# A fused attention and two-MLP kernel: the fill's first eviction, first k load and warm-up matmuls rearranged

## The chip, the cores and the metric

The kernel runs on one core of a Trainium2 chip. The metric is the device time of one execution in microseconds (us); lower is better. A core has engines that work side by side, each through its own queue in order: TensorE (PE in the rows; PEld is its loading of weights), VectorE (DVE), ScalarE (ACT), GpSimd (POOL) and SyncE (SP), which here only issues DMAs.

## The reference, cut to what matters

```python
def _attn_ref(q, k, v):                       # (2, 12, 448, 64) each
    scores = scale * np.matmul(q, k.transpose(0, 1, 3, 2))
    scores = np.where(mask, -1000000000.0, scores)      # causal
    scores = scores - np.max(scores, axis=-1, keepdims=True)
    attn = np.exp(scores)
    attn = attn / (np.sum(attn, axis=-1, keepdims=True) + 1e-09)
    return np.matmul(attn, v).astype(np.float32)
...
def reference(**kwargs):
    ...
    attn_out = _attn_ref(**attn_kwargs)
    x = np.ascontiguousarray(attn_out.transpose(0, 2, 1, 3)).reshape(B * S, H * D)
    x = _moe_ref(x=x, **moe_kwargs)           # silu(x @ w_in) @ w_out, 768 -> 2048 -> 768
    return _moe2_ref(x=x, **moe2_kwargs)      # softmax-linear unit, layer norm, 768 -> 1024 -> 768
```

Attention over 24 heads comes first, then two feed-forward layers over its 896 rows.

## The kernel before

Attention works on 12 pairs of heads, one pair to an iteration `i` of the loop at L342; the loop is software-pipelined. In iteration `i` the scores of pair `i` are computed (`scores`, TensorE, L117 and L109), their row maxima taken (`maxes`, VectorE, L128), and their exponentials with row sums (`exps`, ScalarE, L134). A pair has seven such units, in the order of `UNITS`. One iteration later the pair is normalised (`recip` and `norm`, VectorE and GpSimd, L138 to L146). Two iterations later (`TL = 2`, the pair is called `r`) it is transposed block by block on TensorE into PSUM (`transp`, L157, five groups `g` of up to four blocks) and evicted to SBUF (`evict`: groups 0, 1 and 4 by ScalarE, L175; groups 2 and 3 by VectorE, L173). Three iterations later the product with v follows (`pv`, L186), and one later the result is split into a high and a low part. The schedule is manual: every engine executes in the order in which the code issues.

PSUM holds the transposed groups in a ring of four buffers, tag "x" of the pool `psx`. The warm-up's tile `wp` and the product's tile use the same ring, so group 4 can be transposed only when group 0 has been evicted.

After the loop come four large matrix products on TensorE, with operands split into float32r high and low parts (three matmuls for one product); their weights are streamed in, unpacked and split by the other engines while TensorE works.

The fill is the stretch from the start until the loop runs full. It opens with two memsets on VectorE (L310 clears 448 columns of `xl`, L311 a query tile), `WARM` = 7 matmuls on the cleared columns whose result is not used (L314; 128 weight columns and 448 moving columns, float32r), and `load_pair(0)`, in which SP issues q (L86), k (L87) and two small query tails (L89). The first scores stand behind the warm-up in TensorE's order.

Of the kernel before, what the change touches and what calls it, by code (L numbers as in the profile page):

```python
# [8 lines left out]
F32 = mybir.dt.float32  # L9
# [6 lines left out]
B, H, S, D = 2, 12, 448, 64  # L16
# [12 lines left out]
RAWS = 4  # L29
LAG = 6  # L30
TL = 2
WARM = 7
FEEDS = (8, 10, 11, 12, 12)
GD = (0, 1, 1, 3)
XS = 3
# [7 lines left out]
def fused(ctx, tc, qT, kT, vv, vt, w1, w2, w3, w4, gl, out):  # L43
    nc = tc.nc
    PS = bass.MemoryType.PSUM

    def pool(name, bufs=1, **kw):
        return tc.alloc_tile_pool(name=name, bufs=bufs, **kw)
# [9 lines left out]
    xl = act.tile([128, KD, T], F32R, name="xl", tag="al")  # L58
    g_h, g_l = [None, None], [None, None]

    with tc.manual_schedule():
# [19 lines left out]
        def load_pair(p):  # L81
            b, hp = divmod(p, NP)
            k = att.tile([128, S], F32, name="k32", tag="k32", bufs=QB)
            q = att.tile([128, QC * 128], F32, name="q32", tag="q32", bufs=QB)
            v = att.tile([128, 2, NKB, D], F32, name="v32", tag="v32", bufs=8)
            nc.sync.dma_start(q, qT[b, hp, :, :QC * 128])  # L86
            nc.sync.dma_start(k, kT[b, hp])  # L87
            for j in range(2):
                nc.sync.dma_start(q3s[p % QB][64 * j:64 * j + 64, j], qT[b, hp, 64 * j:64 * j + 64, QC * 128:])  # L89
            raws[p] = (k, q, v)  # L90
# [28 lines left out]
        def ep(p, u):  # L119
            return es[p % EB][:, AT[u]:AT[u] + 4].rearrange("q b k -> q (b k)")[:, :wide(u[1])]  # L120

        def maxes(p, u):
            if p not in st:
                st[p] = att.tile([128, 4, 7], F32, name="st", tag="st", bufs=4)
            o, m = ep(p, u), (mask3 if u[1] == 3 else mask)[:, S - wide(u[1]):]
            if u[1] == 3:
                o, m = (a.rearrange("q (z k) -> q z k", z=2) for a in (o, m))
            nc.vector.tensor_tensor_reduce(  # L128
                o, scs[p, u[0], u[1]], m, -SCALE, 3.0e38,
                ALU.add, ALU.min, st[p][:, 0, COL[u]:COL[u] + 1])  # L130

        def exps(p, u):
            n = COL[u]
            nc.scalar.activation(ep(p, u), ep(p, u), AF.Exp, bias=st[p][:, 0, n:n + 1], scale=-1.0,  # L134
                                 accum_out=st[p][:, 1, n:n + 1])

        def recip(p):
            nc.vector.tensor_scalar(st[p][:, 2], st[p][:, 1], 1e-9, None, ALU.add)  # L138
            nc.vector.reciprocal(st[p][:, 3], st[p][:, 2])

        def norm(p, u, eng):
            r = st[p][:, 3, COL[u]:COL[u] + 1]
            if eng is nc.gpsimd:
                eng.tensor_tensor(ep(p, u), ep(p, u), r.to_broadcast([128, wide(u[1])]), ALU.mult)  # L144
            else:
                eng.tensor_scalar(ep(p, u), ep(p, u), r, None, ALU.mult)  # L146
# [7 lines left out]
        def transp(p, g):  # L154
            t = psx.tile([128, 4, 128], F32, name="tr", tag="x")
            for n, (j, c, kb) in enumerate(GROUPS[g]):
                nc.tensor.transpose(t[:, n], es[p % EB][:, AT[j, c] + kb], ident)  # L157
            trs[p, g] = t

        def evict(p, g):  # L160
            if g == 0:
                aT[p] = att.tile([128, NKB, 2, S], F32, name="aT", tag="aT")
            t, a = trs.pop((p, g)), aT[p]
            if g < 2:
                src, dst = t[:, :QC].rearrange("k c q -> k (c q)"), a[:, 0, g, :QC * 128]
            elif g < 4:
                w = 128 * (4 - g)
                src = t.rearrange("k c q -> k (c q)")[:, :2 * w].rearrange("k (j q) -> k j q", j=2)
                dst = a[:, g - 1, :, QC * 128 - w:QC * 128]
            else:  # L170
                src, dst = t.rearrange("k b (j q) -> k b j q", j=2), a[:, :, :, QC * 128:]
            if g in (2, 3):
                nc.vector.tensor_copy(dst, src)  # L173
            else:
                nc.scalar.activation(dst, src, AF.Copy)  # L175
# [14 lines left out]
        def pv_hi(p):  # L190
            b, hp = divmod(p, NP)
            nc.scalar.activation(xh[:, hp, b * S:b * S + S], pvs[p][:, :S], AF.Copy)

        def pv_lo(p):
            b, hp = divmod(p, NP)
            sl = slice(b * S, b * S + S)
            nc.vector.tensor_tensor(xl[:, hp, sl], pvs[p][:, :S], xh[:, hp, sl].bitcast(F32), ALU.subtract)
# [69 lines left out]
        def feed():  # L267
            m = fed[0]
            fed[0] += 1
            at = lambda a: order[a] if a < len(order) else None  # L270
            if m + 1 < len(order):
                conv_a(*order[m + 1])
            for _ in range(2):
                if len(pend) >= lag[0]:
                    finish(pend.pop(0))
            if m < len(order):
                n, c = order[m]
                conv_b(n, c, x3 if n == 3 else xs, at(m + 1))
                pend.append(m)
            if m + RAWS < len(order):  # L280
                load_w(*order[m + RAWS])
# [25 lines left out]
            nc.vector.tensor_copy(g_h[b][:, f], sg)  # L307
            nc.gpsimd.tensor_tensor(g_l[b][:, f], sg, g_h[b][:, f].bitcast(F32), ALU.subtract)  # L308

        nc.vector.memset(xl[:, 0, :S].bitcast(F32), 0.0)  # L310
        nc.vector.memset(q3s[0], 0.0)  # L311
        wp = psx.tile([128, 512], F32, name="pv", tag="x")
        for _ in range(WARM):
            nc.tensor.matmul(wp[:, :S], xl[:, 0, :128], xl[:, 0, :S], start=True, stop=True)  # L314
        load_pair(0)
        nc.gpsimd.memset(mask, 0.0)
        blk = mask[:, S - 128:]
# [24 lines left out]
        for i in range(NP2 + TL + 2):  # L342
            live = i < NP2
            n, r, p, x = i - 1, i - TL, i - TL - 1, i - TL - 2
            doN, doT, doP, doX = (0 <= a < NP2 for a in (n, r, p, x))
            if doX:
                pv_hi(x)
            if doN:
                exps(n, UNITS[6])
            if live:  # L350
                for _ in range(FEEDS.count(i)):
                    feed()
                for c in (2, 0, 1, 3):
                    scores(i, c)
                for u in UNITS[:2]:
                    maxes(i, u)
                for u in UNITS[:2]:
                    exps(i, u)
            if i == 1:
                for u in UNITS[2:4]:  # L360
                    maxes(i, u)
            late = ()
            if doN:
                recip(n)
                dve = [u for u in KEYS if u[1] < 2] if n == 0 else KEYS if n == NP2 - 1 else KEYS[-1:]
                for u in KEYS:
                    if u not in dve:
                        norm(n, u, nc.gpsimd)
                if n == NP2 - 1:
                    for u in dve:  # L370
                        norm(n, u, nc.vector)
                else:
                    late = dve
            if doX:
                pv_lo(x)
            if live and i != 1:
                for u in UNITS[2:4]:
                    maxes(i, u)
            if doT:
                for g in range(4):  # L380
                    transp(r, g)
                evict(r, 0)
                transp(r, 4)
                evict(r, 1)
            if live:
                for u in UNITS[2:4]:
                    exps(i, u)
                for u in UNITS[4:6]:
                    maxes(i, u)
            if doT:  # L390
                evict(r, 4)
            if doP:
                for z in range(NKB):
                    pv(p, z)
            if live:
                for u in UNITS[4:6]:
                    exps(i, u)
                maxes(i, UNITS[6])
            if doT:
                for g in (2, 3):  # L400
                    evict(r, g)
            for u in late:
                norm(n, u, nc.vector)
            if not live:
                for _ in range(FEEDS.count(i)):
                    feed()
            if live and i + 3 < NP2:
                load_pair(i + 3)
                load_v(i + 3)
            if i == 1:  # L410
                for a in range(RAWS):
                    load_w(*order[a])
            if i == FEEDS[0] - 1:
                conv_a(*order[0])
                shift_w(*order[0])
            if i == NP2 - 1:
                pss.release()
                gm = pool("gm", 2, space=PS, side="right")
            for g in range(4):
                if GD[g] == i - NP2 + 1:  # L420
                    g1drain(g)
# [287 lines left out]
```

## Time and profile before

| | us |
|---|---|
| median of 3 runs | 447.11 (447.08 to 447.6) |
| the profiled execution, its own time | 447.77 |
| its span, first to last instruction | 446.0 |
| TensorE busy in the span | 437.3 |
| VectorE busy | 321.3 |
| ScalarE busy | 224.2 |
| GpSimd busy | 169.5 |

The span lies inside the execution; 1.8 us of the profiled time lie around it. Busy time of TensorE counts a matmul from its start to its end, so a pipelined matmul is counted with its latency. Times within the span count from its first instruction.

### The profile page before, as it was taken

The numbers are of one execution on the slowest core, as the hardware profiler recorded it, in microseconds if no ns is written. First come the engines' busy times: TensorE is split into PE (matmuls) and PEld (weight loads), VectorE is DVE, ScalarE is ACT, GpSimd is POOL, SyncE is SP. The second block draws the span as 40 slices with busy tenths as digits, with TensorE's granted clock in tenths as the row PEclk, the third lists the DMA queues.
The fourth block names the chain that finished last, engine by engine and source line by source line (L and its number), as shares of the span: only waits on it lengthen the run. The fifth ranks groups of instructions, "written<-read, shape, count | busy, mean of one in ns | idle before, by whom it ended". The sixth has DMA issues, their size and how long they took to land.

```text
span 446.0 us, 6961 instructions
## 1 busy us (share of the span) xinstructions
PE 437.3 (98%) x2379; PEld 382.0 (86%) x2379; DVE 321.3 (72%) x705; ACT 224.2 (50%) x519; POOL 169.5 (38%) x189
## 2 busy tenths in 40 slices
PE   8899999999999999999999999999999999999997
PEld 5666666789999999999999999999888888999996
DVE  4978999669999998988775978756878787511110
ACT  4988998444434434344443434433647765712121
POOL 2745656336777666665423324332500000000000
PEclk9999999999999999999999999999999999999999
DMA  5776311205533424242745557564023220010101
GB/s 162 203 252 184 113 47 37 72 0 143 141 102 112 136 77 141 79 135 77 233 142 186 180 144 217 172 209 119 23 71 106 80 63 1 35 37 35 55 35 54
DMA packets 26387, 49.22 MB, mean 110 GB/s; under 512 B 6128, under 2 KB 13936, under 8 KB 26352
## 3 DMA queue, kind: packets, MB, share of 16 engines
q1 hardware_dynamic: 26352, 48.77, 36.6%
q8 instruction: 19, 0.31, 0.3%
q14 instruction: 16, 0.13, 0.1%
HBM read 46.01 MB, written 2.75 MB: 109 GB/s over the span
## 4 chain that ended last, share of the span: by engine, by line
PE 89%; DVE 7%; ACT 3%; issue 0%; DVEq 0%; ACTq 0%
PE h L298 8%; PE h L299 8%; PE h L300 8%; PE h L465 7%; PE h L464 7%; PE h L463 7%; PE ps L631 4%; PE ps L632 4%; PE ps L633 4%; PE h L576 4%; PE h L578 4%; PE h L577 4%; PE pv L186 4%; DVE e L128 3%; PE tr L157 2%; ACT e L134 2%
## 5 line engine op out<-in xcount | busy, mean ns | idle before, releaser
L236 POOL TENSOR_TENSOR wl<-wx,wh 128x384 fp32r<-128x384 f32 x64 | 77.8, 1218 | 98.1 <-ACT wh L235 93.0
L210 ACT ACTIVATE wr<-wr 128x384 f32<-128x384 f32 x96 | 52.7, 554 | 34.0 <-DMA wr<-w_in 33.8
L235 ACT ACTIVATE wh<-wx 128x384 fp32r<-128x384 f32 x64 | 33.4, 522 | 67.8 <-DVE wx L220 30.8
L220 DVE SCALAR_TENSOR_TENSOR wx<-wr,wx 128x384 uint32<-128x384 uint32 x96 | 66.4, 692 | 0.0
L300 PE MATMUL h<-xh,wl 128*128 128x448 f32 x174 | 63.5, 365 | 0.0
L299 PE MATMUL h<-xl,wh 128*128 128x448 f32 x174 | 63.5, 365 | 0.0
L298 PE MATMUL h<-xh,wh 128*128 128x448 f32 x174 | 63.5, 365 | 0.0
L225 DVE TENSOR_SCALAR wr<-wr 128x384 uint32<-128x384 uint32 x96 | 58.5, 609 | 5.0 <-DMA wr<-w_in 4.7
L217 DVE SCALAR_TENSOR_TENSOR wx<-wr 128x384 uint32<-128x384 uint32 x96 | 58.3, 607 | 1.4 <-POOL gl L308 1.3
L465 PE MATMUL h<-gh,wl 128*128 128x448 f32 x160 | 58.3, 364 | 0.0
L463 PE MATMUL h<-gh,wh 128*128 128x448 f32 x160 | 58.2, 364 | 0.0
L464 PE MATMUL h<-gl,wh 128*128 128x448 f32 x160 | 58.2, 364 | 0.0
L308 POOL TENSOR_TENSOR gl<-sg,gh 128x448 fp32r<-128x448 f32 x32 | 41.1, 1286 | 21.5 <-DVE gh L307 10.7
L134 ACT ACTIVATE e<-e,st 128x384 f32<-128x384 f32 (+3 forms) x84 | 43.7, 523 | 9.3 <-DVE st L128 9.1
L144 POOL TENSOR_TENSOR e<-e,st 128x384 f32<-128x384 f32 (+3 forms) x63 | 37.5, 630 | 28.4 <-PE tr L157 17.4
L631 PE MATMUL ps<-w4h,lh 128*128 128x384 f32 (+2 forms) x112 | 38.3, 342 | 0.0
L632 PE MATMUL ps<-w4l,lh 128*128 128x384 f32 (+2 forms) x112 | 37.8, 337 | 0.0
L633 PE MATMUL ps<-w4h,ll 128*128 128x384 f32 (+2 forms) x112 | 37.8, 337 | 0.0
L620 DVE TENSOR_TENSOR ll<-tp,lh 128x512 fp32r<-128x512 f32 x14 | 9.0, 685 | 37.9 <-ACT lh L619 37.9
L299 PEld LDWEIGHTS h<-xl,wh 128*128 128x128 f32 x174 | 32.7, 188 | 2.6
L298 PEld LDWEIGHTS h<-xh,wh 128*128 128x128 f32 x174 | 32.7, 188 | 2.6
L300 PEld LDWEIGHTS h<-xh,wl 128*128 128x128 f32 x174 | 32.7, 188 | 2.6
(99 smaller groups left out, 844.5 us busy)
## 6 DMA issues: line engine op xcount, KB each, us to landing
wr<-w_in SPq DMA_DIRECT2D x96, 384.0 KB, 3.6
k<-kT_in SPq DMA_DIRECT2D x12, 224.0 KB, 2.9
q<-qT_in SPq DMA_DIRECT2D x12, 192.0 KB, 3.1
v<-vv_in SPq DMA_DIRECT2D x12, 192.0 KB, 2.9
out<-o SPq DMA_DIRECT2D x12, 192.0 KB, 1.9
qt<-qT_in SPq DMA_DIRECT2D x24, 16.0 KB, 2.7
v<-vt_in SPq DMA_DIRECT2D x12, 32.0 KB, 2.5
out<-o SPq DMA_DIRECT2D x1, 256.0 KB, 2.0
```

The source lines that it names most:

```text
L217: nc.vector.scalar_tensor_tensor(xu, high, 0x80000000, low, ALU.bitwise_and, ALU.bitwise_or)
L220: nc.vector.scalar_tensor_tensor(xu, high, 3, xu, ALU.logical_shift_left, ALU.bitwise_or)
L225: nc.vector.tensor_scalar(low, low, 29, None, ALU.logical_shift_right)
L236: (lo_engine or nc.gpsimd).tensor_tensor(l, x, h.bitcast(F32), ALU.subtract)
L298: nc.tensor.matmul(ps[:, :S], wh, rh, start=k == 0, stop=False)
L299: nc.tensor.matmul(ps[:, :S], wh, rl, start=False, stop=False)
L300: nc.tensor.matmul(ps[:, :S], wl, rh, start=False, stop=k == KD - 1)
L463: nc.tensor.matmul(ps[:, :S], wh, rh, start=f == 0, stop=False)
L464: nc.tensor.matmul(ps[:, :S], wh, rl, start=False, stop=False)
L465: nc.tensor.matmul(ps[:, :S], wl, rh, start=False, stop=f == KF - 1)
L631: nc.tensor.matmul(ps[:, :w], lh[:, k], w4h[:, k, ns], start=k == 0, stop=False)
L632: nc.tensor.matmul(ps[:, :w], lh[:, k], w4l[:, k, ns], start=False, stop=False)
```

## The change

Four edits, all in the fill.

```diff
-WARM = 7
+WARM = 24
...
-            nc.sync.dma_start(k, kT[b, hp])
+            (nc.scalar if p == 0 else nc.sync).dma_start(k, kT[b, hp])
...
-        nc.vector.memset(xl[:, 0, :S].bitcast(F32), 0.0)
+        nc.vector.memset(xl[:, 0, :128].bitcast(F32), 0.0)
...
-            nc.tensor.matmul(wp[:, :S], xl[:, 0, :128], xl[:, 0, :S], start=True, stop=True)
+            nc.tensor.matmul(wp[:, :128], xl[:, 0, :128], xl[:, 0, :128], start=True, stop=True)
...
                 for u in UNITS[:2]:
                     maxes(i, u)
+                if r == 0:
+                    for g in range(4):
+                        transp(r, g)
+                    evict(r, 0)
                 for u in UNITS[:2]:
                     exps(i, u)
...
             if doT:
-                for g in range(4):
-                    transp(r, g)
-                evict(r, 0)
+                if r > 0:
+                    for g in range(4):
+                        transp(r, g)
+                if r > 0:
+                    evict(r, 0)
+                else:
+                    evict(r, 1)
                 transp(r, 4)
-                evict(r, 1)
+                if r > 0:
+                    evict(r, 1)
```

TensorE's order at the start of the program, in the kernel before (`pv` is the warm-up's tile, `sa` and `sb` the two score tiles of pair 0):

```order
L314 MATMUL pv<-xl 128x448 x7
L117 MATMUL sa<-k_103,q_104 128x384 x2
L117 MATMUL sa<-k_103,q_104 128x128 x2
L117 MATMUL sb<-k_103,q_104 128x256 x2
L109 MATMUL sb<-k_103,qt_86 128x224 x2
```

and in the changed one:

```order
L314 MATMUL pv<-xl 128x128 x24
L117 MATMUL sa<-k_120,q_121 128x384 x2
L117 MATMUL sa<-k_120,q_121 128x128 x2
L117 MATMUL sb<-k_120,q_121 128x256 x2
L109 MATMUL sb<-k_120,qt_86 128x224 x2
```

The scores of pair 0 now stand behind 24 matmuls of 128 columns instead of 7 of 448; the rest of TensorE's order is the same.

ScalarE's order around iteration 2, as a difference (`e_91` is pair 1, `e_92` pair 2, `aT` the evicted transposes of pair 0):

```order
 L134 ACTIVATE e_91,st<-e_91,st 128x256 x2
 L134 ACTIVATE e_91,st<-e_91,st 128x448
+L175 ACTIVATE aT<-tr 128x384
 L134 ACTIVATE e_92,st<-e_92,st 128x384 x2
-L175 ACTIVATE aT<-tr 128x384 x2
+L175 ACTIVATE aT<-tr 128x384
 L134 ACTIVATE e_92,st<-e_92,st 128x128 x2
 L175 ACTIVATE aT<-tr 128x8x64
```

The eviction of group 0 has moved ahead of the first two exponentials of pair 2; the eviction of group 1 stays behind them. Iterations from 3 on are unchanged, and so is VectorE's order but for the smaller memset.

## Rows read from the trace of the kernel before

**Rows 1.** The page: the chain that ended last, its shares of the span by engine.

```profile
PE 89%; DVE 7%; ACT 3%; issue 0%; DVEq 0%; ACTq 0%
```

**Rows 2.** Busy time by stretch, granted clock (PEclk), DMA share, GB/s.

```profile
0.00:21.40 21.40, 17.48 (x99) 12.19 (x99) 15.20 (x70) 15.15 (x52) 10.20 (x29) 1.00 0.65 177
21.40:44.10 22.70, 22.69 (x176) 15.34 (x176) 17.48 (x65) 20.16 (x67) 12.99 (x22) 1.00 0.72 219
```

**Rows 3.** The chain that ended last, from 0 to 26 us: start, duration, what.

```profile
1.39 2.98 PE pv L314 x7
...
6.31 0.56 DVE e L128
...
14.84 1.31 ACT e L134 x4
16.15 0.75 ACT aT L175 x2
...
21.41 0.66 PE tr L157 x4
```

**Rows 4.** Timeline of TensorE: start, duration, line, shape, count, idle before.

```profile
4.30 1.84 PE L117 MATMUL sa<-k,q 64*128 64x384 f32 x8
...
13.90 1.59 PE L157 MATMUL tr<-ident,e 128*128 128x128 f32 x12
16.67 0.63 PE L157 MATMUL tr<-ident,e 128*128 128x128 f32 x4 [1.19 <-ACT aT L175]
17.23 1.14 PE L117 MATMUL sa<-k,q 64*128 64x384 f32 x8
...
18.73 1.02 PE L109 MATMUL sb<-k,qt 128*128 128x224 f32 x4
```

**Rows 5.** The warm-up's line: nanoseconds min/median/max of weight loads and matmuls.

```profile
L314 PEld LDWEIGHTS pv<-xl x7: 287/330/333, 1.4 to 3.4; 128*128 128x128 f32 x7
L314 PE MATMUL pv<-xl x7: 575/575/742, 1.4 to 3.8; 128*128 128x448 f32 x7
```

**Rows 6.** Weight loads by line and shape: busy us, mean ns, idle before.

```profile
L298 PEld LDWEIGHTS h<-xh,wh 128*128 128x128 f32 x174 | 32.7, 188 | 2.6
...
L186 PEld LDWEIGHTS pv<-aT,v 128*64 128x64 f32 x144 | 9.3, 136 | 10.9 <-issue 6.9 <-DVE xl L197 0.5 <-ACT e L134 0.3
```

**Rows 7.** Timeline of TensorE near the end: matmuls of 256 columns.

```profile
442.30 0.28 PE L631 MATMUL ps<-w4h,lh 128*128 128x256 f32 x1
442.42 0.28 PE L632 MATMUL ps<-w4l,lh 128*128 128x256 f32 x1
```

**Rows 8.** Timelines of VectorE, SP and ScalarE at the start.

```profile
0.90 0.43 DVE L310 MEMSET xl<- 128x448 f32 x1 [0.90 <-PEq L700]
1.31 0.17 DVE L311 MEMSET qt<- 128x128 f32 x1
...
1.18 0.42 SPq L87 DMA_DIRECT2D k<-kT_in  x1
...
0.73 1.28 ACT L134 ACT_TABLE_LOAD   x1 [0.73 <-PEq L700]
```

**Rows 9.** DMAs issued in the first 1.6 us: KB, us from issue to landing.

```profile
k<-kT_in SPq DMA_DIRECT2D x1, 224.0 KB, 2.6
```

**Rows 10.** Timeline of ScalarE in iteration 2.

```profile
14.84 0.62 ACT L134 ACTIVATE e<-e,st 128x384 f32<-128x384 f32 x1 [0.61 <-DVE st L128]
...
16.06 0.84 ACT L175 ACTIVATE aT<-tr 128x384 f32<-128x384 f32 x2
...
19.68 0.61 ACT L134 ACTIVATE e<-e,st 128x384 f32<-128x384 f32 x1
```

**Rows 11.** Instructions on the transposed tiles: ns min/median/max.

```profile
L157 PE MATMUL tr<-ident,e x32: 272/272/332, 13.9 to 21.8; 128*128 128x128 f32 x32
L175 ACT ACTIVATE aT<-tr x5: 467/477/581, 16.1 to 21.2; 128x384 f32<-128x384 f32 x4, 128x512 f32<-128x512 f32 x1
```

**Rows 12.** Timeline of VectorE behind iteration 2.

```profile
18.61 0.54 DVE L128 CUSTOM_DVE_ANT_0 e<-sa,mask 128x384 f32<-128x384 f32 x1
```

## The prediction

> **What bounds the kernel now.** The page's chain comes first: TensorE holds 89% of it [rows 1], so only what moves TensorE's start of steady work can count. The table by stretch says where that start is. From 21.4 to 44.1 us TensorE is busy 22.69 of 22.70 us; before 21.4 it is busy 17.48 of 21.40 [rows 2], and all four edits lie there. Then the chain in order of time says who sets that start: warm-up and first scores on TensorE until VectorE's first maximum at 6.31 us, VectorE and ScalarE in turn, from 14.84 us ScalarE alone, until TensorE takes over at 21.41 with group 4 of pair 1's transposes [rows 3]. So the change is worth what it does to two places: when the first scores end (everything to 21.41 hangs on that in a row), and how long ScalarE needs from 14.84 on.
>
> **The change part by part.**
>
> *First eviction ahead of two exponentials.* ScalarE stands idle for 0.61 us until 14.84, when the first maximum of pair 2 lets it go on [rows 10]. Group 0 is the first three transposes of the row at 13.90 [rows 4]. Four transposes in a row take 0.63 us, the last of a stream 0.27 [rows 4, 11], so they start 0.11 apart, and group 0 is in PSUM at 13.90 + 2 x 0.11 + 0.27 = 14.39. Twelve should take 11 x 0.11 + 0.27 = 1.48 and took 1.59, so 0.11 of waits lie among them, and 14.50 is the late bound. Two evictions take 0.84 and one 0.47 [rows 10, 11], so one occupies ScalarE for 0.37. With 0.05 for the signal it runs from 14.44 to 14.81, inside the idle time; on the late bound it ends at 14.92 and costs 0.11 of its gain. Behind 14.84 ScalarE has one eviction less before 21.41: a gain of 0.37, at least 0.26. If that idle time were gone the gain would be nothing, since an eviction would only have changed places with two exponentials. Group 4 of pair 0, which waited 1.19 us for that eviction [rows 4], is done sooner too, but that alone buys nothing: the next scores are then waited for by nobody, since VectorE comes to them at 18.61 [rows 12] and they now start at 17.23 [rows 4]. What is late next is VectorE: the first maximum of pair 3 ends at 18.61 + 0.54 = 19.15, and ScalarE, which takes it at 19.68 [rows 10], will ask for it at 19.31. It is ready, 0.1 us to spare. So the 0.37 reaches 21.41, and TensorE is without a gap behind it.
>
> *k by ScalarE's queue.* k is issued at 1.18 [rows 8] and lands 2.6 later [rows 9], at 3.78; q is issued ahead of it. Issued from ScalarE at the start it lands about 0.45 us sooner, and SP's later DMAs move up by as much. But the scores start at 4.30 [rows 4], behind the warm-up: its first matmul starts at 1.39 [rows 3] and waits 0.742 - 0.575 = 0.17 for its weights, the seven follow 0.373 apart ((2.98 - 0.742) / 6), so its last column goes in at 1.39 + 0.17 + 7 x 0.373 = 4.17, and the scores follow 0.13 later. k was there 0.4 us before; the edit is worth nothing unless the warm-up ends before 3.78. It costs ScalarE one issue, 0.42 us as on SP, ahead of a table load of 1.28 that would then end near 2.4 [rows 8], while the first exponential stands behind the first maximum, which starts at 6.31 [rows 3]: hidden.
>
> *The memset.* 128 columns take 0.17 as the neighbour's, for 0.43 [rows 8]: the warm-up starts at 1.39 - 0.26 = 1.13.
>
> *The warm-up.* Seven matmuls of 448 columns become 24 of 128: 3136 columns become 3072, but weight loads go from 7 to 24. In steps of 448 columns the load (0.33 us by its row, [rows 5]) hides behind the matmul. With 128 it can't. 448 columns in 0.373 us are one column a cycle at 1.2 GHz, the lower of the two levels, so 128 columns stream in 0.107. What a load occupies is read from two rows at the upper level: 128 columns take 0.188 and 64 take 0.136 [rows 6], so 64 columns are 0.052 and 128 are 0.104; matmuls of 256 columns, with one load each, follow 0.12 apart by the printed starts [rows 7], which bounds it from above. At the lower level that is 0.21 to 0.24, twice the matmul's 0.107. I take 0.213. Loads and matmuls overlap, so the pitch is the longer of the two, and 24 cold ones would need 1.30 + 23 x 0.213 = 6.20 to reach the last, for 3.80 (1.56 + 6 x 0.373) now.
>
> The Trainium skill, in "TensorE: Matmul & The Clock Gate", section "LDWEIGHTS (loading the stationary operand)", has a load take its columns divided by 1.2, 107 ns for 128. By that the load would just hide behind the matmul and the warm-up would be shorter than before: the second rival below. This trace disagrees as far as it goes: the same rows have 104 ns at the upper level, and loads of 330 ns cold for 188 warm.
>
> *When the clock rises.* The granted clock reads 1.00 in both stretches [rows 2], but the first rows run at the lower level: the score matmuls of pair 0 take 1.84 us, the same ones of pair 3 take 1.14 [rows 4]. Cold for a time t, and then at double rate, t + 1.14 - t/2 = 1.84 gives t = 1.40: the rise came near 5.70 us, 4.3 after the first warm-up matmul, with TensorE working all that time. If the changed warm-up counts alike, the rise falls between 5.44 (4.3 after 1.13) and 5.70. By then (5.44 - 1.30) / 0.213 = 19.4 to 20.7 pitches have passed, and the other 3.6 to 2.3 take 0.107 each: the 24th starts between 5.83 and 5.95. With its own columns (0.05), the gap (0.13) and scores all at the upper level (1.14) these end between 7.15 and 7.27, for 4.30 + 1.84 = 6.14 now. The first maximum is 1.0 to 1.1 us later, and no slack in the chain to 14.84 takes it up. Scores at full clock win back part of the longer warm-up; that is in the sum.
>
> **The sum.** +1.07 for the warm-up and scores, -0.37 for the eviction, 0 for k: +0.70 us. The profiled execution would go from 447.77 to 448.47, its span from 446.0 to 446.7; that execution stands 0.66 above the median of 447.11, so against the median I say 447.8.
>
> **The rivals.** *Loads of 0.107* (faster side): the 24th starts at 1.30 + 23 x 0.107 = 3.76, the scores at 3.76 + 0.107 + 0.13 = 4.0, with k there at about 3.4. They run cold until 5.44 to 5.70, which does 0.72 to 0.85 of their 1.14, and end at 5.86 to 5.99: -0.15 to -0.28, with the eviction -0.5 to -0.65, so 446.5. For it: the columns are the same in all, and the change reads as if meant so. Against it: the rows on loads above. The change then does what it says, with its k edit at last of use.
>
> *Load and matmul don't overlap at 128 columns*, or a small matmul costs what a 448 one does: pitch 0.32 to 0.373 cold. At 5.57 the 14th or 12th has started, the rest take 0.16 to 0.187 each, the scores end at 8.4 to 9.0: +2.3 to +2.9, net +1.9 to +2.5, so 449.0 to 449.6. For it: no row here has float32r matmuls under 256 columns. Against it: the transposes, 128 columns with a load each, keep 0.11 apart.
>
> *The clock rises late*: half of each pitch has no column streaming, and if the rise waits for the scores, the warm-up is cold to 6.20, the first scores start at 6.4 and are cold (2.28), as are the rest of pair 0's, to some 4.3 us after their start, 10.7. A pair's scores need 2.52 at full clock, the first 1.14 among them (17.23 to 18.73 + 1.02, [rows 4]). By 10.7 half of the 4.3 is done, 2.15, and the rest ends near 11.1, for 6.14 + 1.38 = 7.52 now. That is +3.5; VectorE has earlier maxima to take meanwhile, so I take +3 and net +2.6: 449.7. It decides from a rise later than about 6.0 us, where the scores would end at 7.4 and the net be +0.9. The trace can't tell; in it TensorE streamed without a pause before the rise.
>
> **How the numbers follow.** The likeliest, loads that bound the pitch and a rise as now, 0.56, spans 447.5 to 448.1 on its own (loads of 0.104 or 0.12 at the upper level, an eviction gain of 0.26 or 0.37, the rise 0.3 us either way). Loads of 0.107: 0.17. No overlap: 0.13. Late clock: 0.14. The range from 446.3 to 449.5 holds the first two, most of the third and a mild form of the last. About 0.2%, 0.9 us, is what a measurement of this kernel can tell from no change. The likeliest passes +0.9 in a third of its cases: slower 0.18 + 0.12 + 0.13 = 0.43; faster only from the far end of the first rival and what I don't see, 0.07; the rest 0.50.
>
> **What would show it.** The warm-up row: 24 matmuls from 1.13, and loads there near 0.33 us whose ends lie 0.21 apart; the first scores in 1.14 from about 6.0 and the first maximum near 7.3; ScalarE's eviction of group 0 in the gap before the first exponential of pair 2, with 0.37 less between that exponential and group 4 of pair 1; steady TensorE from about 22.1. The prediction is wrong if the warm-up's matmuls start 0.11 apart, if the first scores take over 1.5 us, or if the gap ahead of pair 2's first exponential is gone.

## The result and the profile after

The changed kernel takes 450.16 us (median of 6 runs, 449.71 to 450.88), the kernel before 447.5 beside it (6 runs, 447.08 to 448.19): a ratio of 1.0055, 95% interval 1.0044 to 1.0066, or 2.66 us more. In the longer series below some executions lie 2 to 3 us above the others of their kernel (7 of 31 of the kernel before in the first series), which pulls at the ratios more than at the medians, so medians are compared there.

The profiled execution, 449.71 us, is the fastest of the six, and the one before took 447.77; so the two traces are 1.94 apart, where the medians are 2.66 apart. Its span is 447.9 us for 446.0. The chain that ended last, in order of time (start, duration, what), against [rows 3]:

```profile
1.05 5.38 PE pv L314 x24
6.44 2.03 PE sa L117 x8
...
8.62 0.56 DVE e L128
...
16.73 0.49 ACT aT L175
17.22 1.24 ACT e L134 x4
...
23.34 0.66 PE tr L157 x4
```

The first maximum starts 2.31 us later (8.62 for 6.31), TensorE's steady work 1.93 later (23.34 for 21.41), and the span is 1.9 longer: all of it was lost before the first maximum, and 0.38 was won back between it and 23.34. Where the loss came from stands in TensorE's timeline (start, duration, line, shape, count), against [rows 4], and in the warm-up's own line (nanoseconds min/median/max), against [rows 5]:

```profile
6.37 2.08 PE L117 MATMUL sa<-k,q 64*128 64x384 f32 x8
8.24 0.78 PE L117 MATMUL sb<-k,q 64*128 64x256 f32 x4
8.94 1.02 PE L109 MATMUL sb<-k,qt 128*128 128x224 f32 x4
10.14 1.14 PE L117 MATMUL sa<-k,q 64*128 64x384 f32 x8 [0.17 <-DVE st L128]
```

```profile
L314 PEld LDWEIGHTS pv<-xl x24: 288/333/338, 1.1 to 5.9; 128*128 128x128 f32 x24
L314 PE MATMUL pv<-xl x24: 415/415/476, 1.1 to 6.0; 128*128 128x128 f32 x24
```

The 24 matmuls take 5.38 us in all; less the last one's 0.415 and the first one's delay of 0.06 (0.476 - 0.415), 23 steps are 4.90, so they start 0.213 apart, the pace taken for loads at the lower level, and none was faster at the end. The first scores then start at 6.37 and are cold, which here means at the lower of TensorE's two levels, from beginning to end: 2.08 us, for 1.84 before and 1.14 for the same work of pair 1. The next ones (0.78 for 0.60) are partly cold, the ones after that are not: the clock rose near 8.6 us, behind the warm-up. The table of clock changes stored with each trace says the same: its first entry at full clock stands at 8.59 us, and at 5.76 in the trace before. The granted clock of a stretch does not show this (it reads 1.00 for 1.05 to 6.37 us as well), so the level has to be read from durations or from that table.

ScalarE around the early eviction, against [rows 10]:

```profile
16.35 0.18 ACT L134 ACTIVATION_READ_ACCUMULATOR e<-e,st 128x1 f32 x1
16.73 0.49 ACT L175 ACTIVATE aT<-tr 128x384 f32<-128x384 f32 x1 [0.20 <-PE tr L157]
17.14 0.62 ACT L134 ACTIVATE e<-e,st 128x384 f32<-128x384 f32 x1
```

```profile
17.03 0.08 DVE L128 DVE_READ_ACCUMULATOR2_ANT st<- 128x1 f32 x1
```

The maximum that the exponential needs is there at 17.11 (17.03 + 0.08), and the exponential starts at 17.14: the eviction stands whole in the gap. And the DMAs issued in the first 1.6 us (KB, us to landing), against [rows 9]:

```profile
k<-kT_in ACTq DMA_DIRECT2D x1, 224.0 KB, 3.5
q<-qT_in SPq DMA_DIRECT2D x1, 192.0 KB, 3.3
```

k, issued at 0.73 by ScalarE, needs 3.5 us for 2.6 and lands at 4.2, later than the 3.78 it had from SP's queue.

### The profile page after: what moved, and what is told of

Its sections match the earlier page's. It is cut to its first block, busy times and chain, and to the rows that moved or that the text cites. A ratio compares the mean times of both kernels' runs of the same rounds, so it can differ in the third digit from the quotient of the medians.

```text
span 447.9 us, 6995 instructions
## 1 busy us (share of the span) xinstructions
PE 440.4 (98%) x2396; PEld 385.5 (86%) x2396; DVE 321.8 (72%) x705; ACT 224.1 (50%) x519; POOL 170.0 (38%) x189
## 4 chain that ended last, share of the span: by engine, by line
PE 90%; DVE 6%; ACT 3%; issue 0%; DVEq 0%; ACTq 0%
PE h L298 8%; PE h L300 8%; PE h L299 8%; PE h L474 7%; PE h L473 7%; PE h L472 7%; PE ps L640 4%; PE ps L642 4%; PE ps L641 4%; PE h L586 4%; PE h L585 4%; PE h L587 4%; PE pv L186 4%; DVE e L128 3%; PE tr L157 2%; ACT e L134 2%
## 5 line engine op out<-in xcount | busy, mean ns | idle before, releaser
L220 DVE SCALAR_TENSOR_TENSOR wx<-wr,wx 128x384 uint32<-128x384 uint32 x96 | 67.4, 702 | 0.0
```

Source lines behind the costliest of these rows:

```text
L220: nc.vector.scalar_tensor_tensor(xu, high, 3, xu, ALU.logical_shift_left, ALU.bitwise_or)
```

## The experiments

Two theories of the loss. **Half-filled**: the changed warm-up's columns stream in only half of the time, since each load takes twice as long as its columns, and behind such a warm-up the clock rises later than behind one whose columns stream without gaps. **Length**: the kind of warm-up makes no difference, and the scores merely stand behind a longer one. Each edit is against the kernel before unless said otherwise; warm-ups work on zeros and their results are not used, so all of these kernels compute the reference.

**Old warm-up, the other edits kept.** The changed kernel with

```diff
-WARM = 24
+WARM = 7
...
-        nc.vector.memset(xl[:, 0, :128].bitcast(F32), 0.0)
+        nc.vector.memset(xl[:, 0, :S].bitcast(F32), 0.0)
...
-            nc.tensor.matmul(wp[:, :128], xl[:, 0, :128], xl[:, 0, :128], start=True, stop=True)
+            nc.tensor.matmul(wp[:, :S], xl[:, 0, :128], xl[:, 0, :S], start=True, stop=True)
```

> The changed kernel with the old warm-up (7 matmuls of 448 columns, 448 columns cleared); the early eviction and k by ScalarE's queue stay. If the warm-up alone made the change slow, this is 0.37 us faster than the kernel before (0.26 to 0.37 from the eviction, nothing from k): ScalarE evicts group 0 in the gap before the first exponential of pair 2, TensorE's group 4 of pair 1 at about 21.0. Rival, the early eviction or the split queues cost something too: same as before or slower.

447.65 us (10 runs), the kernel before 447.88 (31 runs): 0.23 less, ratio 0.9996, 0.9967 to 1.0024, which by itself is no proof of a gain. The trace shows one; its chain has

```profile
6.01 0.56 DVE e L128
...
14.11 0.49 ACT aT L175
...
20.73 0.66 PE tr L157 x4
```

From the first maximum to TensorE's steady work 14.72 us, for 15.10 before: 0.38. The first maximum itself comes 0.3 earlier behind the same warm-up: the clock table has the rise at 5.14. Nothing in these two edits costs what the change lost.

**The new warm-up alone.**

```diff
-WARM = 7
+WARM = 24
...
-        nc.vector.memset(xl[:, 0, :S].bitcast(F32), 0.0)
+        nc.vector.memset(xl[:, 0, :128].bitcast(F32), 0.0)
...
-            nc.tensor.matmul(wp[:, :S], xl[:, 0, :128], xl[:, 0, :S], start=True, stop=True)
+            nc.tensor.matmul(wp[:, :128], xl[:, 0, :128], xl[:, 0, :128], start=True, stop=True)
```

> The kernel before with the new warm-up alone (24 matmuls of 128 columns, 128 columns cleared). Both theories of the warm-up's loss: the changed kernel's +2.7 us and the eviction's 0.37 that is now missing, +3.0 us in all. If it is +2.7 or less, the eviction gained nothing.

450.85 us (10 runs) against 447.88 (ratio 1.0071, 1.0039 to 1.0103): +2.97, as expected, and 0.31 more than the whole change lost. TensorE again goes cold into the scores:

```profile
6.37 2.08 PE L117 MATMUL sa<-k,q 64*128 64x384 f32 x8
8.23 1.06 PE L117 MATMUL sb<-k,q 64*128 64x256 f32 x4
9.22 1.02 PE L109 MATMUL sb<-k,qt 128*128 128x224 f32 x4
```

**As long as before, but half filled.** 13 matmuls of 128 columns in place of 7 of 448:

```diff
-WARM = 7
+WARM = 13
...
-            nc.tensor.matmul(wp[:, :S], xl[:, 0, :128], xl[:, 0, :S], start=True, stop=True)
+            nc.tensor.matmul(wp[:, :128], xl[:, 0, :128], xl[:, 0, :128], start=True, stop=True)
```

> The kernel before with 13 warm-up matmuls of 128 columns in place of 7 of 448, so that the warm-up ends at 4.3 us, nearly as before (13 x 0.213 = 2.77 for 7 x 0.373 = 2.61), with its columns in half of the time only. Theory half-filled (such matmuls do not bring the clock's rise, only columns without pauses do): the first scores start near 4.45 and stay at the lower level throughout (2.0 us or more for 1.84), the rest of pair 0's too, rise near 8, +0.5 to +1.5 us. Theory length (the rise does not depend on the kind of warm-up, the loss is that the scores stand behind a longer one): +0.1 us.

448.74 us (10 runs) against 447.88: +0.86 for a warm-up that ends as before's does. The ratio, 1.0006 with 0.9984 to 1.0028, holds no change as well; but all ten lie at 448.26 or above, and of the 31 of the kernel before 24 lie at 448.25 or below. In the trace

```profile
1.39 3.04 PE L314 MATMUL pv<-xl 128*128 128x128 f32 x13 [1.39 <-DVE xl L310]
4.35 2.08 PE L117 MATMUL sa<-k,q 64*128 64x384 f32 x8
6.22 1.06 PE L117 MATMUL sb<-k,q 64*128 64x256 f32 x4
7.21 1.38 PE L109 MATMUL sb<-k,qt 128*128 128x224 f32 x4
```

the scores start at 4.35 for 4.30 and are cold throughout, and what follows is cold to 7.96, where the clock table has the rise, 2.2 us later than before. Length is out as the only cause; half-filled forecast this.

**Longer, with columns all the time.** `WARM = 14`, of 448 columns.

> The kernel before with 14 warm-up matmuls of 448 columns for 7: longer, but with columns all the time. Theory half-filled: the rise comes within the warm-up near 5.7 as before, the last 3 matmuls take 0.19 each, the scores start near 6.4 and take 1.14: +1.4 us. Theory length, where the rise is a matter of chance and not of the warm-up: scores partly cold as with 24 small ones, about +2 us or more.

449.56 us (10 runs) against 447.88 (ratio 1.0033, 1.0006 to 1.0060): +1.7, between the two forecasts.

```profile
1.39 5.60 PE L314 MATMUL pv<-xl 128*128 128x448 f32 x14 [1.39 <-DVE xl L310]
6.91 1.39 PE L117 MATMUL sa<-k,q 64*128 64x384 f32 x8
```

In this execution the clock rose only at 7.46, behind the whole warm-up, though columns streamed from 1.56 on; the kernel before, with the same columns up to 4.2, had it at 5.76. So the moment of the rise differs where the kind of warm-up does not, and length costs something too. Still, a warm-up that holds the scores back 0.5 us longer than 24 small matmuls do costs 1.3 us less.

**Many loads, columns all the time.** 12 matmuls of 256 columns:

```diff
-WARM = 7
+WARM = 12
...
-            nc.tensor.matmul(wp[:, :S], xl[:, 0, :128], xl[:, 0, :S], start=True, stop=True)
+            nc.tensor.matmul(wp[:, :256], xl[:, 0, :128], xl[:, 0, :256], start=True, stop=True)
```

> The kernel before with a warm-up of 12 matmuls of 256 columns (448 columns still cleared): load and columns take the same 0.213 us, so columns stream without pauses, 3072 of them in 2.56 us as 7 x 448. Theory half-filled (the rise needs columns without pauses): no change, within 0.2 us of before. Rival, many loads or many small matmuls are what delays the rise or costs time: slower by 0.5 us or more.

447.94 us against 447.82 (10 and 31 runs; ratio 1.0001, 0.9992 to 1.0011): no change that these runs can tell. In the trace the first scores are cold only at their start:

```profile
4.24 1.24 PE L117 MATMUL sa<-k,q 64*128 64x384 f32 x8
```

Twelve float32r loads did no harm where the columns hid them.

**The same 24 small matmuls in bfloat16.**

```diff
-        nc.vector.memset(xl[:, 0, :S].bitcast(F32), 0.0)
+        wz = att.tile([128, 128], mybir.dt.bfloat16, name="wz", bufs=1)
+        nc.vector.memset(wz, 0.0)
...
-            nc.tensor.matmul(wp[:, :S], xl[:, 0, :128], xl[:, 0, :S], start=True, stop=True)
+            nc.tensor.matmul(wp[:, :128], wz, wz, start=True, stop=True)
```

> The kernel before with 24 warm-up matmuls of 128 columns on a cleared bfloat16 tile of its own, in place of float32r: the same count and columns as in the change. If the float32r load is what halves the pace, these start 0.107 us apart, end about 0.5 us sooner than before's, columns stream without pauses, and the time is that of before or up to 0.4 us under it. Rival, small matmuls as such do not bring the rise: scores cold as in the change, +0.5 us or more.

447.47 us against 447.82 (10 and 31 runs): -0.35, at the fast end of what was expected; the interval of the ratio (0.9996, 0.9981 to 1.0011) holds no change as well.

```profile
0.99 2.74 PE L315 MATMUL pv<-wz 128*128 128x128 bf16 x24 [0.99 <-DVE wz L311]
4.02 1.30 PE L117 MATMUL sa<-k,q 64*128 64x384 f32 x8 [0.29 <-DMA k<-kT_in]
```

```profile
L315 PEld LDWEIGHTS <-wz x24: 105/152/152, 1.0 to 3.3; 128*128 128x128 bf16 x24
L315 PE MATMUL pv<-wz x24: 289/314/314, 1.0 to 3.4; 128*128 128x128 bf16 x24
```

A load by the row takes 0.152 us for 0.333, and 23 steps fit in 2.74 - 0.29: 0.107 apart, one column a cycle at the lower level. The same count of the same size did no harm once the load was hidden. The scores now wait for k, 0.29 us.

**Next to no warm-up.** One matmul of 128 columns.

> The kernel before with a single warm-up matmul of 128 columns: the scores start when k is there, near 3.85 us, and nothing precedes them. If half-filled warm-up matmuls count nothing towards the rise, this is like the run with 13 of them (448.7 us median), 0.2 to 0.5 us better for its earlier scores. If they count in part, the rise comes later here than there and it is slower than that run, +1.0 to +2 us on the kernel before.

448.62 us against 447.82 (10 and 31 runs; ratio 1.0024, 1.0010 to 1.0038): +0.80, like the 13 small ones' +0.86. The scores start at 3.94, 0.4 us before theirs, are cold for longer, and it comes to the same:

```profile
3.94 2.08 PE L117 MATMUL sa<-k,q 64*128 64x384 f32 x8 [2.08 <-DMA k<-kT_in]
5.78 1.09 PE L117 MATMUL sb<-k,q 64*128 64x256 f32 x4
6.80 1.86 PE L109 MATMUL sb<-k,qt 128*128 128x224 f32 x4
```

The forecast for "count nothing" was 0.2 to 0.5 better than 448.7, for "count in part" +1 or more; it lies between, so whether they count for a little stays open. The clock tables hint that they do: the rise came at 9.11 here, 5.2 us after the scores' start, and in the three traces with half-filled float32r warm-ups 2.2 to 3.6 us after it; one execution of each does not decide it. In time 13 half-filled matmuls were worth no more than one.

**bfloat16 with the other two edits.** The changed kernel with 20 bfloat16 matmuls.

> The changed kernel (early eviction, k by ScalarE's queue) with 20 warm-up matmuls of 128 columns in bfloat16: they start near 1.05, 0.107 us apart, and end near 3.35, when k lands. Theory half-filled: columns without pauses from 1.2 us on, the rise some 0.3 us sooner than before, scores from 3.5: 0.37 for the eviction and 0.3 to 0.6 for the fill, 0.7 to 1.0 us faster than the kernel before. Rival, small matmuls as such delay the rise: slower than before.

448.13 us against 447.82 (10 and 31 runs; ratio 1.0008, 0.9999 to 1.0018): the forecast of 0.7 to 1.0 us faster was wrong. TensorE's timeline, of the slowest of the ten executions, shows where:

```profile
0.99 2.32 PE L315 MATMUL pv<-wz 128*128 128x128 bf16 x20 [0.99 <-DVE wz L311]
4.19 2.08 PE L117 MATMUL sa<-k,q 64*128 64x384 f32 x8 [0.89 <-DMA k<-kT_in]
6.06 1.06 PE L117 MATMUL sb<-k,q 64*128 64x256 f32 x4
7.05 1.86 PE L109 MATMUL sb<-k,qt 128*128 128x224 f32 x4
```

I had k land at 3.35; from ScalarE's queue it lands at 4.15. TensorE pauses 0.89 us, all of pair 0's scores are cold, and the clock rises at 9.66.

**The pause filled, and k back on SP.** The last kernel with 28 matmuls instead of 20, and with 24 and `nc.sync.dma_start(k, kT[b, hp])`:

> The run with 20 bfloat16 warm-up matmuls, early eviction and k by ScalarE's queue, with 28 of them, so that the warm-up reaches to 4.05 us and meets the scores at 4.2, where the other one paused 0.89 us for k. If the pause is what delayed the clock's rise there, the first scores end near 5.6 and it is 0.3 to 0.6 us faster than the kernel before, for 0.3 us slower with the pause. If it was chance, no better than that one.

> The early eviction and the bfloat16 warm-up of 24 small matmuls, with k on SP's queue again (its tile of 128 columns in place of the cleared part of xl). If the gains add, 0.37 for the eviction and 0.35 for the earlier scores: 0.7 us faster than the kernel before, a span near 445. Rival, the eviction is worth nothing once the fill is faster: 0.35 us faster.

With 28: 447.47 us against 447.8 (11 and 21 runs; ratio 0.9992, 0.9983 to 1.0000), -0.33 for +0.31 with the pause. So eight more matmuls in the pause were worth 0.64; whether because TensorE did not pause or because more columns stood ahead of the scores, these two runs do not separate. The trace is not the one forecast, with first scores that end near 5.6:

```profile
4.18 2.08 PE L117 MATMUL sa<-k,q 64*128 64x384 f32 x8
6.05 1.06 PE L117 MATMUL sb<-k,q 64*128 64x256 f32 x4
7.04 1.02 PE L109 MATMUL sb<-k,qt 128*128 128x224 f32 x4
```

In this execution (447.71, slower than the median) the first scores are cold all the same, and the clock rises at 6.98, 6.0 us after the warm-up's start.

With 24 and k on SP: 447.24 us against 447.8 (11 and 21 runs), -0.56 by the medians, the best of this study and between its two forecasts; the interval of the ratio (0.9997, 0.9984 to 1.0010) does not separate it from the kernel before. The eviction did not bring its full 0.37 in the traces of these two runs, where the first scores are cold. ScalarE with 28 matmuls:

```profile
14.76 0.49 ACT L175 ACTIVATE aT<-tr 128x384 f32<-128x384 f32 x1 [0.41 <-PE tr L157]
15.14 0.60 ACT L134 ACTIVATE e<-e,st 128x384 f32<-128x384 f32 x1
```

The maximum for this exponential was there at 14.93 (VectorE's read of it ends then), so the eviction held the exponential up by 0.2 us; with 24 it is the same (14.70 and 14.94).

**The change itself, its warm-up filled.** All that sets this off from the changed kernel is the type, on a cleared tile of its own, and the count that makes it as long: 47 bfloat16 matmuls, 47 x 0.107 for 24 x 0.213.

> The changed kernel with 47 warm-up matmuls of 128 columns in bfloat16 for its 24 in float32r: 47 x 0.107 = 5.0 us at the lower level, as long as those (24 x 0.213), and columns all the time instead of half of it. Everything else is the change. Theory half-filled: the clock rises within or soon after the warm-up, so that the scores take about 1.1 to 1.6 us for 2.08 and start no later than 6.2: 0.3 to 1.0 us slower than the kernel before, where the change is 2.7 slower. Theory length: cold scores from 6.2, 2 us or more slower, like the change.

448.37 us against 447.58 (12 and 18 runs; ratio 1.0016, 1.0007 to 1.0025): +0.79, where the change lost 2.66.

```profile
0.99 4.43 PE L315 MATMUL pv<-wz 128*128 128x128 bf16 x47 [0.99 <-DVE wz L311]
5.35 1.14 PE L117 MATMUL sa<-k,q 64*128 64x384 f32 x8
```

Here the clock rose within the warm-up, at 4.45: the warm-up ends at 5.42 us, for some 6.2 at one pace, and the scores run at full speed. (This execution, 447.77, is one of the faster: five of the twelve lie under 448.0 and seven between 448.26 and 448.96.) By the medians some 1.9 of the change's 2.66 us are the half-filled warm-up's, and 0.8 are its length less the eviction's gain.

## Why the prediction was wrong

- *What bounds the kernel*: right. What the first maximum lost and what ScalarE gained add up to the span's difference, 2.31 - 0.38 = 1.93.
- *The pace of the loads*: right. 0.213 us was read from loads at the upper level and a doubling, and measured 0.213. The 107 ns of the Trainium skill ("TensorE: Matmul & The Clock Gate", section "LDWEIGHTS (loading the stationary operand)") do not hold for float32r here; bfloat16 steps of 0.107 do not contradict them. The rival that goes with them is the first of the list, not the second as the text has it.
- *The rise*: this is the step that failed: "If the changed warm-up counts alike, the rise falls between 5.44 (4.3 after 1.13) and 5.70." It did not count alike. The rise came at 8.59, the scores started at 6.37 for the forecast 6.0 to 6.1 and took 2.08 for 1.14, and the first maximum was 2.31 us late in the profiled execution instead of 1.07. Of the 1.24 too much, 0.3 are the warm-up's last steps at the lower level and 0.94 the cold scores. The runs with 13 small matmuls, with 256 columns, with bfloat16 and with 47 of them show why: the float32r loads left half of the time without a column, and where columns filled that time, with the same count or the same length, most of the loss was gone.
- *The rival that came true* was "The clock rises late", net +2.6 against 2.66 measured. It had a chance of 0.14 and was the only one for which I wrote "The trace can't tell"; the range's upper end of 449.5 cut it off. That its price came out is in part luck: it had the rise at 10.7 (measured 8.59) and the end of pair 0's scores 3.5 us late, rounded to 3, where the trace has 2.4 (8.94 + 1.02 for 7.52); and the price fits the medians better than the profiled execution (+1.9). What makes the medians differ by 0.7 more than the two traces do is not shown.
- *The eviction*: 0.37 forecast, 0.38 in two traces (this one and the run with the old warm-up). Right; what it says of a gap that is gone showed in the runs with 24 and 28 bfloat16 matmuls, where 0.2 of the gain was lost. By medians it is 0.23 and 0.31, neither clear of the noise. The transposes ahead of it start 0.12 apart by the row used ((0.63 - 0.27) / 3), not 0.11, which moves the eviction by 0.02 and changes nothing.
- *k by ScalarE's queue*: the sum of 0 was right because the warm-up covered it, but its reason was wrong. It was to land 0.45 us sooner and landed 0.4 later. Without the cover, in the run with 20 bfloat16 matmuls, TensorE waited 0.89 us for it.

## What to carry to other kernels

What paid in these runs was a warm-up with columns streaming, not one with instructions running. With float32r, 128 columns did not hide the load of 128 weight columns (steps of 0.213 us for 0.107 of columns), while 256 columns did, and bfloat16 hid it with 128. Look first at what a warm-up is worth: a single matmul in its place cost 0.80 us here, the half-filled one 2.97. Let it reach up to the first real matmul and no further (14 x 448 cost 1.7). Pauses of 0.25 and 0.29 us behind 24 bfloat16 matmuls cost nothing that the medians show; 20 with a pause of 0.89 were 0.64 slower than 28 without.

Moving a load to a second queue starts it sooner, and it may still land later, as k did; read the landing, not the issue.

## What the runs showed of the hardware

*With q and k on two queues both landed later.* With q and k issued at the same time from SP and ScalarE, and SP's next loads moved up, q needed 3.1 to 3.3 us for 2.4 and k 3.3 to 3.5 for 2.6, from issue to landing, in three traces (the changed kernel, the old warm-up, 20 bfloat16 matmuls). With k on SP behind q and a bfloat16 warm-up they needed 2.4 and 2.7. Whether the two delay each other or the loads behind them delay both is not shown.

*The moment of the rise differs between executions.* From the clock tables of the traces, one execution of each kernel, in us:

| warm-up | it starts | first scores start | clock rises |
|---|---|---|---|
| 7 x 448 (before) | 1.39 | 4.30 | 5.76 |
| 7 x 448, early eviction, k by ScalarE | 1.38 | 4.29 | 5.14 |
| 14 x 448 | 1.39 | 6.91 | 7.46 |
| 12 x 256 | 1.38 | 4.24 | 4.50 |
| 24 bfloat16 | 0.99 | 4.02 | 4.38 |
| 24 bfloat16, early eviction | 0.98 | 3.97 | 6.84 |
| 28 bfloat16 | 0.98 | 4.18 | 6.98 |
| 47 bfloat16 | 0.99 | 5.35 | 4.45 |
| 20 bfloat16, pause 0.89 | 0.99 | 4.19 | 9.66 |
| 24 float32r (changed) | 1.05 | 6.37 | 8.59 |
| 24 float32r alone | 1.05 | 6.37 | 9.16 |
| 13 float32r | 1.39 | 4.35 | 7.96 |
| one float32r | 1.38 | 3.94 | 9.11 |

The first eight, with columns streaming and no pause over 0.29 us, have the rise 3.1 to 6.1 us after the warm-up's start, and the three half-filled ones 6.6 to 8.1. Within the first eight the first scores were cold for all of their 2.08 us in two traces, for part in five (1.84, 1.54, 1.39, 1.30, 1.24) and not at all in one (1.14). The first two have the same warm-up and differ by 0.6. The runs of one kernel spread over about 1 us (449.71 to 450.88 for the changed one), of the size that such a spread would give; that it is the reason is not shown.
